# One-core attention, gated convolution and mixer kernel: first mixture's weight cast moved to VectorE, its loads booked later, later heads' preparation issued behind the first head's rows

## Chip, cores and metric

The kernel runs on 1 core of one Trainium2 chip. The metric is the device time of one execution in microseconds (us). Before the change it was 816.27 us, the median of 3 runs (811.01 to 820.26).

## What is computed

Three stages follow one another, all in fp32 on 4 batches of 576 tokens:

```
scores = q @ k.T / 8 + min(-(cum_i - cum_j), 0), causal      # 8 heads x 4 batches, cum = cumsum(max(s, 0))
attn   = softmax(scores);  x = attn @ v                      # (4, 576, 512)
h      = max(x @ w_in, 0);  c = 3-tap depthwise conv of h over tokens
x      = (h * sigmoid(c)) @ w_out                            # "first mixture", 512 -> 1024 -> 512
u      = x + U,V mixing of the tokens (rank 32)
out    = u + max(u @ w_ch1, 0) @ w_ch2                       # 512 -> 2048 -> 512
```

The weights of the mixtures are float64 in HBM, and the core turns them into fp32 pairs (a high part and a remainder) itself.

## The kernel before, in words

**A planner sets the order.** The Python code first collects operations with an engine, a cost in ns, and the buffers read and written (`Plan.op`). `Plan.order` (L219 on) then runs a list schedule: it keeps a clock for each engine (PE = TensorE, DVE = VectorE, ACT = ScalarE, POOL = GpSimd, SP, which issues the DMAs), takes the engine that is free first, and issues its ready operation with the lowest program number. An operation is ready when all its predecessors (`preds`) are done by this bookkeeping: end of the predecessor, plus a latency between the two engines, plus the predecessor's `late`. For a DMA on SP `late` is worked out from its bytes (one shared wire, 360 bytes per ns). The result is a fixed order for each engine; on the chip each engine works through its own list in that order and waits on semaphores. So an instruction that waits for data holds up all that stands behind it on its engine, whatever the planner believed. SP too issues its DMAs in order, and a DMA that reuses one of eight completion semaphores waits until the DMA that had it before has landed.

**The heads.** `att_head(h)` (L1317) is called for each of the 32 heads (`NH`) in turn: it asks for the loads of the next head (`prep_v`, `prep4`, `prep`, `place`), then plans scores (`scores`, `scores4`), softmax, transposes (`transp`) and the product with v (`av`). Heads 0 to 7 (`FS`) use plain fp32 products: `prep4` (L576) loads q and k into a tile `qkF` and puts the head's row of `cc` (the running sum of s) into it by two small DMAs, called "the head's rows" below (`qkF<-cc`). From head 8 on, q and k of two heads are loaded together into two tiles `t` (`prep`, L599), split by POOL (L356) and DVE (L362) into high and low parts, and copied by DMA into `qkA` and `qkB` (`place`, L617); the rows then come from a scratch tensor `r_d` in HBM, which `decay_parts` (L462) fills once: DVE splits `cc` into the tile `ws`, and four DMAs write `r_d` (two from `ws`, two of ones). `clear` (L479) zeroes the two `qkB` tiles on POOL.

**The first mixture's weights.** There are 16 slices of 128x512 (`w1_jobs`): eight of `w_in` (`w1h`, `w1l`) and eight of `w_out` (`w1o`). For each, `load_split` (L527) plans the load of 512 KB (`raw_w<-w_in`, L530) into a ring of two buffers, `decode64` (ACT Prelu L504 on the raw tile, then DVE L511 and L520, which give fp32), the high part as an ACT cast (`hi_act`, L353) and the low part as a DVE subtraction (`lo_dve`, L362). `st["first"]` is head 0's row DMA; the loads of `load_split` have it as a predecessor.

**Around the start.** SP issues s, q/k of head 0, v, the mask and the identity (`ident`, three DMAs) before head 0's rows, because the planner sees those as ready earlier; DVE clips and sums s (L459, L460), and in the order before also splits `cc` for `r_d` there. `h == 1` is the call of `att_head` in which `decay_parts` and `clear` are asked for.

**PSUM.** Scores, transposes, av products and the mixtures share eight banks; a bank is given to the next user when its last reader is done, so PE can wait for an ACT copy that empties a bank of another kind (`x<-av`, L843).

Of the kernel before, what the change touches and what calls it, by code (L numbers as in the profile page):

```python
# [42 lines left out]
AHEAD = 80  # L43

RECIP = (3,)

CAPS = dict(sc=3, pt=1, av=5, h=4, y=4, tp=2, t1=4, mh=1, ma=8, my=8, mx=2)

# [89 lines left out]
class Op:  # L138

    def __init__(self, eng, cost, fn, n, late):  # L140
        self.eng, self.cost, self.fn, self.n, self.late = eng, cost, fn, n, late
        self.preds = set()


class Plan:
# [36 lines left out]
    def order(self):  # L182
# [46 lines left out]
        while True:  # L229
# [47 lines left out]
            late = o.late  # L277
            if e == "SP":
                wire = max(wire, t + 1400) + o.late
                late = wire + 980 - end  # L280
            self.busy[e] += o.cost
            out.append((t, len(out), o))
            for b in holds.get(o, ()):
# [25 lines left out]
def tile_attention_moe_mixer(  # L309
# [149 lines left out]
    dve(S, lambda: nc.vector.tensor_scalar(cum(), cum(), 0.0, 8.0, ALU.max, ALU.mult), key, key, True)  # L459
    scan = dve(S, lambda: nc.vector.tensor_tensor_scan(cum(), cum(), cum(), 0.0, ALU.add, ALU.max), key, key)  # L460

    def decay_parts():  # L462
        hi_dve(lambda: rk[:, 0, :], cum, key, [(rk, 0)], S)
        lo_dve(lambda: rk[:, 1, :], cum, lambda: rk[:, 0, :], [*key, (rk, 0)], [(rk, 1)], S)
        for i in range(2):
            dma(
                147456,
                lambda i=i: nc.sync.dma_start(out=f32(r_t[:, i:4:2, 1 - i, :]), in_=f32(rk())),
                [rk],
                [(r_d, i)],  # L470
            )
            dma(
                147456,
                lambda i=i: nc.sync.dma_start(out=f32(r_t[:, i:4:2, i, :]), in_=one_d[i]),
                [],
                [(r_d, 2 + i)],
            )

    def clear(t):  # L479

        o = pool(2 * S, lambda: nc.gpsimd.memset(f32(t[0:64]), 0.0), [], [(t, "r"), (t, "q")], extra=0)
        o.preds.add(scan)

    for t in p4s:
        o = pool(64, lambda t=t: nc.gpsimd.memset(t[:, S:640], 0.0), [], [(t, "pad")], extra=0)
        o.preds.add(scan)


    def decode64(out, okeys, raw, n):

        def half(i, dt):
            return raw().bitcast(dt).rearrange("p (n two) -> p n two", two=2)[:, :n, i]

        def oi():
            return out().bitcast(I32)  # L500

        act(
            n,
            lambda: nc.scalar.activation(half(1, F32), half(1, F32), ACTF.Prelu, scale=2.0**-111, alpha=2.0**32),  # L504
            [raw],
            [(raw, 1)],
            40,
        )
        dve(
            n,  # L510
            lambda: nc.vector.tensor_scalar(  # L511
                oi(), half(1, I32), 3, None, ALU.logical_shift_left
            ),
            [(raw, 1)],
            okeys,
            True,
        )
        dve(
            n,
            lambda: nc.vector.scalar_tensor_tensor(  # L520
                oi(), half(0, I32), 29, oi(), ALU.logical_shift_right, ALU.bitwise_or
            ),
            [(raw, 1), *okeys],
            okeys,
        )

    def load_split(src, h, l, c, n, name, lo=lo_pool):  # L527

        raw = ring(dec, "raw", RINGS["w64"], [128, 512], I64, f"raw_{name}")
        load = dma(n * 1024, lambda: nc.sync.dma_start(out=raw[:, :n], in_=src[:, c : c + n]), [], [raw])  # L530
        load.preds.add(st["first"])
        wf = ring(dec, "wf", RINGS["wf"], [128, 512], F32, f"wf_{name}")
        decode64(lambda: wf[:, :n], [wf], raw, n)
        hi_act(lambda: h[:, :n], lambda: wf[:, :n], [wf], [h], n)
        lo(lambda: l[:, :n], lambda: wf[:, :n], lambda: h[:, :n], [wf, h], [l], n)

    def load_cw():
# [61 lines left out]
    def prep(h):  # L599

        t1 = ring(ap, "t1", RINGS["qkh"], [128, 2, S], F32R, f"t1_{h}")
        t2 = ring(ap, "t2", RINGS["qkh"], [128, 2, S], F32R, f"t2_{h}")

        for c, (hi, lo) in enumerate(((t1, t2), (t2, t1))):

            def raw(c=c, lo=lo):
                return f32(lo[:, c, :])

            dma(294912, lambda c=c, raw=raw: nc.sync.dma_start(out=raw(), in_=qk[h // 2, :, c]), [], [(lo, c)])
            hi_pool(lambda c=c, hi=hi: hi[:, c, :], raw, [(lo, c)], [(hi, c)], S)  # L610
            lo_dve(
                lambda c=c, lo=lo: lo[:, c, :],
                raw,
                lambda c=c, hi=hi: hi[:, c, :],
                [(lo, c), (hi, c)],
                [(lo, c)],
                S,  # L617
            )
        st["pair", h // 2] = (t1, t2)
# [685 lines left out]
    hi_dve(lambda: mask[:, 384:512], lambda: mraw[:, 0:128], [mraw], [(mask, 1)], 128)  # L1305
    hi_dve(lambda: mask[:, 736:800], lambda: mraw[:, 128:192], [mraw], [(mask, 2)], 64)
    dma(65536, lambda: nc.sync.dma_start(out=ident[:, 0:128], in_=ident_d), [], [(ident, 0)])

    for a in (0, 64):
        dma(  # L1310
# [2 lines left out]
            [],  # L1313
            [(ident, 1 + a)],
        )

    w1_jobs = [(f, c) for c in (0, 512) for f in range(NF1)]  # L1317

    def att_head(h):

        if h + 1 < NH:
# [4 lines left out]
            else:  # L1326
                if h % 2 == 1:
                    prep(h + 1)
                place(h + 1)
        if h == 1:  # L1330
            decay_parts()
            for t in qkBs:
                clear(t)
# [48 lines left out]
    for h in range(NH + 1):  # L1382
# [10 lines left out]
        att_head(h)  # L1393
        for n, (f, c) in enumerate(w1_jobs):
            if h == W1_AT[n]:
                load_split(w1[f], w1h[f, c], w1l[f, c], c, 512, f"w1_{f}_{c}", lo_dve)
        if h == CW_AT:
            load_cw()
        if h == MIX_AT:
# [180 lines left out]
```

## Time and profile before

| | before |
|---|---|
| median of 3 runs | 816.27 us |
| the profiled execution, its own time | 813.74 us |
| its span, first to last instruction | 811.9 us |
| mean granted TensorE clock | 0.995 |
| TensorE busy | 788.5 us (97%) |
| ACT busy / DVE busy / POOL busy | 464.1 / 471.8 / 182.3 us |
| moved by DMA | 119.69 MB, mean 147 GB/s |

The profile is of one execution, 813.74 us long, of which 811.9 us lie between the first and the last instruction. Times of rows are us from the start of that span. "Busy" is time in which an engine executes; a row's bracket, [idle before <-releaser], is how long the engine sat idle before it and which engine's work or which DMA ended that. PEclk is the mean clock granted to TensorE as a share of its upper level: 1.00 is 2.4 GHz and 0.50 is 1.2 GHz.

### The profile page before, as it was taken

To read this page: it belongs to the slowest core of one execution; us is meant where nothing else is said; L and a number is where in the kernel's file an instruction comes from. 1 tells how busy PE (TensorE), PEld (TensorE's weight loads), DVE (VectorE), ACT (ScalarE), POOL (GpSimd) and SP (SyncE) were. 2 spreads that over 40 slices of the span, in tenths; PEclk is the share of its full clock that TensorE was granted. 3 is DMA by queue.
4 is the path that set the end of the run, shared out by engine and by line. 5 is a ranking of instruction groups with operands and counts; after the bars stand their busy time and mean duration, and the time that the engine had idled before them with its cause. 6 is when DMAs were issued, how large, how long until landed. Compare 5 with 4: busy or idle time off the path is not lost.

```text
span 811.9 us, 15176 instructions
## 1 busy us (share of the span) xinstructions
PE 788.5 (97%) x5300; PEld 708.5 (87%) x5300; DVE 471.8 (58%) x1152; ACT 464.1 (57%) x1176; POOL 182.3 (22%) x291
## 2 busy tenths in 40 slices
PE   4899999999999999999999999999999999999998
PEld 2556798998899998999999999999998888888888
DVE  6686886635855368547888957444576232323232
ACT  4688998758868488776667445444455222222221
POOL 3444564633446245241220000000000000000000
PEclk9899999999999999999999999999999999999999
DMA  7657755644555256230226346455578363636343
GB/s 215 174 161 216 208 144 136 161 111 101 154 135 142 69 114 194 45 111 1 91 79 207 136 153 213 147 174 187 165 246 294 95 201 97 198 101 188 111 123 98
DMA packets 66309, 119.69 MB, mean 147 GB/s; under 512 B 9396, under 2 KB 34868, under 8 KB 66232
## 3 DMA queue, kind: packets, MB, share of 16 engines
q1 hardware_dynamic: 66160, 118.70, 50.5%
q8 instruction: 42, 0.69, 0.4%
q14 instruction: 35, 0.29, 0.1%
q10 hardware_dynamic: 72, 0.01, 0.0%
HBM read 68.81 MB, written 28.90 MB: 120 GB/s over the span
## 4 chain that ended last, share of the span: by engine, by line
PE 90%; DMA 5%; ACT 3%; DVE 1%; issue 1%; POOL 0%; SPq 0%; DVEq 0%; ACTq 0%; POOLq 0%
PE my L1261 24%; PE ma_A L1161 16%; PE y L916 13%; PE h L874 12%; PE ma_S L1161 6%; PE sc L681 6%; PE pt L804 5%; PE av L830 5%; DMA raw_w<-w_in 2%; PE tp L933 1%; DMA qkF<-cc 1%; PE t L952 1%; ACT P L659 1%; DMA r_d<-ws 1%; DMA qkA<-t 1%
## 5 line engine op out<-in xcount | busy, mean ns | idle before, releaser
L1261 PE MATMUL my<-mh,w 128*128 128x512 f32 (+1 forms) x560 | 159.2, 368 | 0.0
L1161 PE MATMUL ma_A<-u,W 128*128 128x288 f32 x960 | 138.2, 295 | 0.0
L1161 PEld LDWEIGHTS ma_A<-u,W 128*128 128x128 f32 x960 | 131.4, 188 | 0.5 <-ACT p L1175 0.2
L1239 ACT ACTIVATE mh<-ml 128x512 fp32r<-128x512 f32 (+1 forms) x80 | 47.2, 589 | 137.5 <-DMA ml<-ch_d 79.2
L1261 PEld LDWEIGHTS my<-mh,w 128*128 128x128 f32 x560 | 101.7, 189 | 17.5
L1242 DVE SCALAR_TENSOR_TENSOR ml<-ml,mh 128x512 fp32r<-128x512 f32 (+1 forms) x80 | 50.6, 638 | 112.8 <-ACT mh L1239 112.6
L916 PE MATMUL y<-gh,w1o 128*128 128x288 f32 x512 | 113.4, 300 | 0.0
L1261 PE MATMUL my<-ml,w 128*128 128x512 f32 (+1 forms) x280 | 103.1, 368 | 0.0
L670 POOL TENSOR_SCALAR P<-P,sm 128x128 f32<-128x128 f32 (+3 forms) x128 | 75.5, 606 | 91.9 <-DVE sm L733 64.3
L642 DVE CUSTOM_DVE_ANT_0 sc<-sc,mask 128x128 f32<-128x128 f32 (+2 forms) x144 | 69.1, 498 | 38.4 <-PE sc L681 36.0
L916 PEld LDWEIGHTS y<-gh,w1o 128*128 128x128 f32 x512 | 85.3, 188 | 0.5
L874 PE MATMUL h<-xh,w1h 128*128 128x290 f32 x256 | 79.7, 311 | 0.1
L886 DVE SCALAR_TENSOR_TENSOR c<-h,cw,c 128x288 f32<-128x288 f32 x128 | 64.2, 513 | 24.3 <-ACT c L882 23.3
L874 PE MATMUL h<-xl,w1h 128*128 128x290 f32 x256 | 76.5, 299 | 0.0
L874 PE MATMUL h<-xh,w1l 128*128 128x290 f32 x256 | 76.3, 298 | 0.0
L916 PE MATMUL y<-gl,w1o 128*128 128x288 f32 x256 | 75.3, 294 | 0.0
L1175 ACT COPY s<-ma_A 128x288 f32<-128x288 f32 x96 | 38.2, 400 | 64.2 <-PE ma_A L1161 55.0
L659 ACT ACTIVATE P<-sc,sm 128x128 f32<-128x128 f32 (+3 forms) x128 | 68.2, 537 | 9.8 <-DVE sm L642 6.1
L365 POOL TENSOR_TENSOR gl<-c,gh 128x288 fp32r<-128x288 f32 x64 | 52.7, 829 | 92.7 <-ACT gh L901 79.4
L353 ACT COPY th<-pt 128x384 f32<-128x384 f32 (+2 forms) x128 | 63.8, 498 | 9.3 <-PE pt L804 8.5
L804 PE MATMUL pt<-ident,P 128*128 128x128 f32 x320 | 60.3, 276 | 1.0 <-ACT P L659 0.9
L1261 PEld LDWEIGHTS my<-ml,w 128*128 128x128 f32 x280 | 52.8, 189 | 8.6
(135 smaller groups left out, 1528.4 us busy)
## 6 DMA issues: line engine op xcount, KB each, us to landing
ml<-ch_d SPq DMA_DIRECT2D x64, 256.0 KB
ch_d<-s SPq DMA_DIRECT2D x64, 144.0 KB
raw_w<-w_in SPq DMA_DIRECT2D x16, 512.0 KB
raw_w2a<-w_in SPq DMA_DIRECT2D x16, 512.0 KB
raw_w2b<-w_in SPq DMA_DIRECT2D x16, 512.0 KB
t<-qk_in SPq DMA_DIRECT2D x24, 288.0 KB
qkB<-t SPq DMA_DIRECT2D x24, 288.0 KB
qkA<-t SPq DMA_DIRECT2D x24, 288.0 KB
```

Source lines behind the costliest of these rows:

```text
L353: act(n, lambda: nc.scalar.copy(out(), src()), r, w)
L365: pool(n, lambda: nc.gpsimd.tensor_tensor(out(), src(), f32(hi()), ALU.subtract), r, w, two=True)
L642: lambda: nc.vector.tensor_tensor_reduce(out=ps[:rows, :w], in0=ps[:rows, :w], in1=mask[:rows, m0 : m0 + w], scale=-0.125, scalar=3.0e38 i ...
L659: lambda: nc.scalar.activation(out(), ps[:rows, :w], ACTF.Exp, bias=low(), scale=-1.0, accum_out=total()),
L670: lambda: nc.gpsimd.tensor_scalar(t[:, :w], t[:, :w], r(), 1.0, ALU.mult, ALU.mult),
L804: nc.tensor.transpose(pt[:, o + rows - 128 : o + rows], d["P"][i][:, 128 * j : 128 * j + 128], turn)
L874: nc.tensor.matmul(ps[:, :W], lhsT=ww, rhs=xx, start=kt + n == 0, stop=kt == KT - 1 and n == 2)
L886: lambda k=k: nc.vector.scalar_tensor_tensor(c(), hh[:, k : k + HS], cw[:, 3 * f + k : 3 * f + k + 1], c(), ALU.mult, ALU.add),
L916: nc.tensor.matmul(ps[:, :HS], lhsT=ww, rhs=xx(), start=f + n == 0, stop=f == NF1 - 1 and n == 2)
L1161: nc.tensor.matmul(ps[:, :HS], lhsT=ww, rhs=uu, start=first and k == 0, stop=k == 5, skip_group_check=True)
L1242: lambda: nc.vector.scalar_tensor_tensor(ml[:, :n], raw(), 0.0, f32(mh[:, :n]), ALU.max, ALU.subtract),
L1261: nc.tensor.matmul(ys[c][dt][:, :n], lhsT=ww, rhs=xx[:, :n], start=f + k == 0, stop=f == NF2 - 1 and k == 2)
```

## The change

Four things are done. (1) The high part of the 16 slices of the first mixture is cast on DVE (`hi_dve`) in place of ACT (`hi_act`). (2) For those slices the planner books the load 3 x 400 ns later and the Prelu's result 400 ns later (`SLACK`); no instruction is added, only the planner's idea of when things are ready moves. (3) `decay_parts` and `clear` are asked for in `att_head(4)`, not `att_head(1)`, and are tied to the last PE operation planned by then (`after_pe`); the loads of head 8's and 9's q and k get the 25th last PE operation as a predecessor. (4) The three identity DMAs get head 0's row DMA as a predecessor.

```diff
+SLACK = 400
...
             if e == "SP":
                 wire = max(wire, t + 1400) + o.late
-                late = wire + 980 - end
+                late = wire + 980 - end + o.slack
...
+    def after_pe(o, back=1):
+        o.preds.add([x for x in plan.ops if x.eng == "PE"][-back])
+
     def decay_parts():
         hi_dve(lambda: rk[:, 0, :], cum, key, [(rk, 0)], S)
+        after_pe(plan.ops[-1])
...
                 [(r_d, 2 + i)],
             )
+            after_pe(plan.ops[-1])
...
         o = pool(2 * S, lambda: nc.gpsimd.memset(f32(t[0:64]), 0.0), [], [(t, "r"), (t, "q")], extra=0)
-        o.preds.add(scan)
+        after_pe(o)
...
-    def decode64(out, okeys, raw, n):
+    def decode64(out, okeys, raw, n, slack=0):
...
             40,
-        )
+        ).late = slack
...
-    def load_split(src, h, l, c, n, name, lo=lo_pool):
+    def load_split(src, h, l, c, n, name, lo=lo_pool, slack=0):
...
         load.preds.add(st["first"])
+        load.slack = 3 * slack
...
-        hi_act(lambda: h[:, :n], lambda: wf[:, :n], [wf], [h], n)
+        (hi_dve if slack else hi_act)(lambda: h[:, :n], lambda: wf[:, :n], [wf], [h], n)
...
             dma(294912, lambda c=c, raw=raw: nc.sync.dma_start(out=raw(), in_=qk[h // 2, :, c]), [], [(lo, c)])
+            if h == len(FS):
+                after_pe(plan.ops[-1], 25)
...
     dma(65536, lambda: nc.sync.dma_start(out=ident[:, 0:128], in_=ident_d), [], [(ident, 0)])
+    plan.ops[-1].preds.add(st["first"])
...
-        if h == 1:
+        if h == 4:
             decay_parts()
...
-                load_split(w1[f], w1h[f, c], w1l[f, c], c, 512, f"w1_{f}_{c}", lo_dve)
+                load_split(w1[f], w1h[f, c], w1l[f, c], c, 512, f"w1_{f}_{c}", lo_dve, SLACK)
```

Since a list schedule decides, the whole order of the first heads shifts. On PE the rows differ up to the product `y_0_2` of the first mixture's first half-batch (its rows after the 656th); the 3190 rows behind it read alike in both programs.

The first place is SP's queue at the start, up to the rows of head 2 (third head). `cc` is the running sum, `qkF_104` and `qkF_129` are the tiles of even and odd heads, `vr` holds v, `raw_w_f_c` is slice f of the weights, `t_8` belongs to heads 8 and 9. Before:

```order
L584 DMA qkF_129<-cc 1x16x36
L596 DMA vr_165<-vP_in 128x640
L530 DMA raw_w_0_0_169<-w_in 128x512
L468 DMA r_d<-ws 64x1x576
L474 DMA r_d<-one_in 64x576
L468 DMA r_d<-ws 64x1x576
L474 DMA r_d<-one_in 64x576
L530 DMA raw_w_1_0_198<-w_in 128x512
L609 DMA t_8_204<-qk_in 128x576
L582 DMA qkF_104<-qk_in 64x1152
L584 DMA qkF_104<-cc 1x16x36
L589 DMA qkF_104<-cc 1x16x36
```

And now:

```order
L591 DMA qkF_129<-qk_in 64x1152
L605 DMA vr_141<-vP_in 128x640
L593 DMA qkF_104<-cc 1x16x36
L593 DMA qkF_129<-cc 1x16x36
L1318 DMA ident<-ident_in 128x128
L1324 DMA ident<-ident_in 128x64 x2
L538 DMA raw_w_0_0_177<-w_in 128x512
L538 DMA raw_w_1_0_184<-w_in 128x512
L591 DMA qkF_104<-qk_in 64x1152
L593 DMA qkF_104<-cc 1x16x36
L598 DMA qkF_104<-cc 1x16x36
```

The four `r_d` writes and the load of `t_8` no longer stand between head 0 and head 2; q and k of head 1 and the second v tile now stand ahead of head 0's rows, where only the identity stood.

The second place is SP's queue further on, where these writes and loads stand now: behind the rows of head 5 (`qkF_129`), ahead of slice 6 and of q, k and rows of head 6 (`qkF_104`).

```order
L591 DMA qkF_129<-qk_in 64x1152
L593 DMA qkF_129<-cc 1x16x36
L598 DMA qkF_129<-cc 1x16x36
L481 DMA r_d<-one_in 64x576 x2
L475 DMA r_d<-ws 64x1x576 x2
L538 DMA raw_w_6_0_506<-w_in 128x512
L591 DMA qkF_104<-qk_in 64x1152
L593 DMA qkF_104<-cc 1x16x36
L598 DMA qkF_104<-cc 1x16x36
L618 DMA t_8_562<-qk_in 128x576
L618 DMA t_8_573<-qk_in 128x576
L640 DMA qkB_457<-r_d 4x1152
```

Before, the same stretch of the queue held this:

```order
L530 DMA raw_w_6_0_461<-w_in 128x512
L582 DMA qkF_129<-qk_in 64x1152
L584 DMA qkF_129<-cc 1x16x36
L589 DMA qkF_129<-cc 1x16x36
L530 DMA raw_w_7_0_542<-w_in 128x512
L530 DMA raw_w_0_512_562<-w_in 128x512
L582 DMA qkF_104<-qk_in 64x1152
L584 DMA qkF_104<-cc 1x16x36
L589 DMA qkF_104<-cc 1x16x36
L596 DMA vr_615<-vP_in 128x640
```

The slices fall behind by one or two, and the `r_d` writes and `t_8` loads take their place.

The third place is ACT around the copy `x_0<-av_1` that empties the bank of the first av product (L843 before, L854 now). `P` and `p` are softmax rows, `th` transposed rows, `raw_w` the Prelu of a slice. Before:

```order
L353 COPY th_0_416<-pt_0_391 128x384
L353 CAST w1h_420<-wf_w_3_0_374 128x512
L659 ACTIVATE P_0_425,sm_212<-sc_0_386,sm_212 128x128
L659 ACTIVATE P_1_430,sm_212<-sc_1_397,sm_212 128x256
L504 ACTIVATE raw_w_4_0_376<-raw_w_4_0_376 128x512
L843 COPY x_0_363<-av_1_403 128x320
L353 CAST xh_0_106<-x_0_363 128x576
L353 COPY th_1_451<-pt_1_438 128x512
```

And now:

```order
L670 ACTIVATE P_1_385,sm_199<-sc_1_355,sm_199 128x256
L356 COPY th_0_398<-pt_0_378 128x384
L512 ACTIVATE raw_w_3_0_301<-raw_w_3_0_301 128x512
L670 ACTIVATE P_2_404,sm_199<-sc_2_367,sm_199 128x384
L854 COPY x_0_347<-av_1_387 128x320
L356 CAST xh_0_106<-x_0_347 128x576
L356 COPY th_1_425<-pt_1_408 128x512
L512 ACTIVATE raw_w_4_0_369<-raw_w_4_0_369 128x512
```

Slice 4's Prelu, which stood directly ahead of that copy, now stands behind it, slice 3's stands ahead of it in its place, and the cast of slice 3 has left ACT.

## Rows read from the trace of the kernel before

**Rows 1.** The page: span and busy time of each engine.

```profile
span 811.9 us, 15176 instructions
...
PE 788.5 (97%) x5300; PEld 708.5 (87%) x5300; DVE 471.8 (58%) x1152; ACT 464.1 (57%) x1176; POOL 182.3 (22%) x291
```

**Rows 2.** Windows: stretch, length, busy PE, PEld, DVE, ACT, POOL; PEclk, DMA share, GB/s.

```profile
8.40:50.00 41.60, 34.80 (x180) 21.86 (x182) 28.15 (x90) 30.00 (x85) 18.37 (x25) 0.92 0.71 205
50.00:100.00 50.00, 45.63 (x307) 33.30 (x304) 39.21 (x122) 44.00 (x128) 24.60 (x36) 1.00 0.70 200
100.00:155.00 55.00, 55.00 (x425) 50.04 (x424) 37.64 (x115) 46.44 (x138) 30.13 (x46) 1.00 0.61 147
155.00:812.00 657.00, 653.09 (x4395) 603.25 (x4394) 361.15 (x821) 342.78 (x827) 105.90 (x167) 1.00 0.47 140
21.80:25.10 3.30, 3.30 (x10) 2.54 (x11) 1.37 (x6) 1.25 (x4) 1.95 (x4) 0.50 0.44 93
38.80:42.20 3.40, 3.40 (x13) 2.83 (x12) 2.56 (x10) 2.67 (x8) 1.34 (x2) 0.50 0.54 148
...
35.00:65.00 30.00, 26.24 (x156) 17.10 (x154) 21.46 (x67) 24.31 (x67) 13.45 (x20) 0.94 0.57 172
35.40:37.90 2.50, 0.07 (x2) 0.02 (x1) 0.35 (x2) 1.01 (x3) 0.00 (x0) 1.00 0.95 282
```

**Rows 3.** Timeline of PE, 0 to 90 us: start, length, instruction [idle before <-releaser].

```profile
18.78 0.33 PE L804 MATMUL pt<-ident,p 128*128 128x128 f32 x1 [1.35 <-POOL p L670]
...
21.79 1.62 PE L681 MATMUL sc<-qkF 128*128 128x128 f32 x4 [2.24 <-DMA qkF<-cc]
...
37.88 1.19 PE L681 MATMUL sc<-qkF 128*128 128x512 f32 x2 [2.42 <-ACT x L843]
...
48.53 0.71 PE L697 MATMUL sc<-qkF 128*64 128x288 f32 x4
...
53.36 0.91 PE L681 MATMUL sc<-qkF 128*128 128x384 f32 x2 [0.79 <-ACT x L843]
...
56.32 0.39 PE L681 MATMUL sc<-qkF 128*128 128x128 f32 x2
...
69.61 1.77 PE L681 MATMUL sc<-qkF 128*128 128x384 f32 x4 [1.00 <-ACT x L843]
```

**Rows 4.** The chain that ended last, in order of time: start, length, what.

```profile
6.24 1.82 DMA qkF<-cc
9.01 5.86 DMA r_d<-ws
14.90 6.76 DMA qkF<-cc
...
30.15 6.63 DMA raw_w<-w_in
...
153.34 1.20 PE y L916 x9
```

**Rows 5.** Timeline of ACT, 8 to 100 us: Prelus that waited for their slice.

```profile
36.86 0.65 ACT L504 ACTIVATE raw_w<-raw_w 128x512 f32<-128x512 f32 x1 [2.78 <-DMA raw_w<-w_in]
...
52.33 0.67 ACT L504 ACTIVATE raw_w<-raw_w 128x512 f32<-128x512 f32 x1 [1.33 <-DMA raw_w<-w_in]
...
68.59 0.66 ACT L504 ACTIVATE raw_w<-raw_w 128x512 f32<-128x512 f32 x1 [1.48 <-DMA raw_w<-w_in]
```

**Rows 6.** Waits of SP's queue, 0 to 30 us: us in total, times, longest.

```profile
SPq L1312 <- DMA qkF<-qk_in: 1.7, 1, 1.7
```

**Rows 7.** Groups by shape, 0 to 155 us: busy us, mean ns.

```profile
L511 DVE TENSOR_SCALAR wf_w<-raw_w 128x512 int32<-128x512 int32 x16 | 8.8, 553 | 8.0 <-ACT raw_w L504 8.0
...
L353 ACT CAST w1h<-wf_w 128x512 fp32r<-128x512 f32 x8 | 5.1, 641 | 0.2 <-DVE wf_w L520 0.2
...
L481 POOL MEMSET qkB<- 64x1152 f32 x2 | 2.0, 1053 | 0.0
```

**Rows 8.** Line L359, VectorE's casts: ns min/median/max, first and last start.

```profile
L359 DVE CAST ws<-cc x1: 447/447/447, 5.6 to 5.6; 32x576 fp32r<-32x576 f32 x1
```

More of the change, by code (lines that the diff above doesn't have):

```diff
@@ L141, in __init__ @@
         self.eng, self.cost, self.fn, self.n, self.late = eng, cost, fn, n, late
+        self.slack = 0
         self.preds = set()
@@ L531, in load_split @@
         load.preds.add(st["first"])
+        load.slack = 3 * slack
         wf = ring(dec, "wf", RINGS["wf"], [128, 512], F32, f"wf_{name}")
-        decode64(lambda: wf[:, :n], [wf], raw, n)
-        hi_act(lambda: h[:, :n], lambda: wf[:, :n], [wf], [h], n)
+        decode64(lambda: wf[:, :n], [wf], raw, n, slack)
+        (hi_dve if slack else hi_act)(lambda: h[:, :n], lambda: wf[:, :n], [wf], [h], n)
         lo(lambda: l[:, :n], lambda: wf[:, :n], lambda: h[:, :n], [wf, h], [l], n)
@@ L1315, in tile_attention_moe_mixer @@
         )
+        plan.ops[-1].preds.add(st["first"])
     w1_jobs = [(f, c) for c in (0, 512) for f in range(NF1)]
```

## Prediction

> **What bounds the kernel now.** I first read the busy shares: TensorE works 788.5 of 811.9 us [rows 1], so 23.4 us without work is all that a new order can win, besides stretches at a lower clock. The windows say where they lie [rows 2]: 8.4 us at the start, before the first product, 6.8 us between 8.4 and 50 (41.60 - 34.80), 4.4 us between 50 and 100, none between 100 and 155, 3.9 us in the 657 us behind that. PE's last row that the change moves is in the product `y_0_2`, which ends at 153.34 + 1.20 = 154.5 [rows 4]; behind it the order is the same and PE has work nearly without a gap, so what is won or lost before 154.5 should reach the end one for one.
>
> Then the timeline of PE, for the gaps one by one [rows 3]: 1.35 (a softmax row still on POOL), 2.24 (the rows of head 2), 2.42, 0.79 and 1.00 (each time a bank that an ACT copy had yet to empty), together 7.8 of the 11.2 us lost between 8.4 and 100. Two of them cost more than their length: from 21.80 for 3.30 us and from 38.80 for 3.40 us, each right behind a gap of over 2 us, the granted clock is 0.50, the lower of its two levels, with PE busy throughout [rows 2]. That is 1.65 and 1.70 us more.
>
> Last, what those gaps waited for. The rows of head 2 are 2.2 KB, and took 6.76 us from issue to landing at 14.90; in front of them SP's queue holds an `r_d` write that took 5.86 us [rows 4], with three more like it, a slice of weights and `t_8`. The three ACT copies were late because a Prelu ahead of them in ACT's order waited for its slice: 2.78, 1.33 and 1.48 us at 36.86, 52.33 and 68.59 [rows 5]. The first slice took 6.63 us from its issue at 30.15 [rows 4]. So these waits of PE are waits for DMAs, passed on by ACT.
>
> **The change part by part.** The sum is made against the profiled execution (813.74 us, 1.8 of it outside its span); it lies 2.5 us under the median of the runs, and I add that difference at the end.
>
> *The start.* Head 0's rows now stand behind head 1's q and k and the second v tile, 608 KB, where the identity's 128 KB stood. An issue of SP can wait for an earlier landing: the second identity DMA waited 1.7 us for q and k [rows 6]. The 480 KB more are 1.7 us at the 282 GB/s of 35.4 to 37.9 [rows 2] if nothing hides them, and nothing if the rows wait for the running sum anyway. ACT issued its two row DMAs at 6.24 and they landed in 1.82 [rows 4]. The identity, which moves behind, is first used by the transposes, behind the scores of heads 0 and 1, and DVE loses two operations (one is the cast of 447 ns [rows 8]) ahead of the mask. I take -0.6 us (0 to -1.7).
>
> *The `r_d` writes and `t_8` leave the start.* Ahead of head 2's rows only two slices, q and k are left. The gap of 2.24 and the slow clock behind it should go: +3.9 us (0 to 3.9). The 1.35 us for POOL I leave where they are (0 to +1.35): a score product now stands in that gap, but the same softmax row ends it.
>
> *The first late slice.* The load is booked 1.2 us and the Prelu 0.4 us later, 1.6 of the 2.78 us that it was late. The rest: `t_8`'s copies to the two `qkB` tiles, 576 KB, went into the queue directly ahead of it and now don't, 2.0 us at 282 GB/s. In the new order slice 3's Prelu, not slice 4's, stands ahead of the copy. So +2.42 + 1.70 = +4.1 us (0 to 4.1).
>
> *The two later ones.* 1.33 and 1.48 are both under 1.6, but the moved traffic falls near them; half of 0.79 + 1.00, +0.9 us (0 to 1.8).
>
> *What the moved work meets.* Four `r_d` writes (576 KB), two loads and two copies of `t_8` (1152 KB), 1.7 MB, now go between head 5's and head 8's loads. That is 6.3 us at 282 GB/s; from 35 to 65 the DMA engines are busy 0.57 of 30 us [rows 2], which leaves 13. It fits on the mean, not at every place. The queue is in order, and slice 6 and q, k and rows of head 6 stand directly behind the writes. I take -1.0 us, like one of the smaller gaps of rows 3; the bound is a gap like head 2's with its clock, -3.9. The zeroing of `qkB`, 2 x 1.05 us on POOL [rows 7], now stands ahead of head 3's softmax rows; POOL is busy 18.4 of the 41.6 us there [rows 2], so 0, and -2.1 if that cover is gone.
>
> *The cast.* ACT loses 16 x 0.64 = 10.3 us [rows 7]. DVE's cast of 128x512 isn't in the trace. Between the 447 ns of 32x576 [rows 8] and the 553 of a 128x512 operation with one input [rows 7] I take the second, which has the shape: 16 x 0.55 = 8.8 us. On PE by itself 0 (+1.0 to -1.5).
>
> *The pace.* When PE waits less, ACT and DVE must do the same work in less time. From 8.4 to 50 DVE is busy 28.2 us; with 5 casts 30.9, in 33.6 us instead of 41.6, 92%. ACT falls from 30.0 to 26.8, 80%. The nearest stretch with an engine that full is 50 to 100: ACT 88%, and PE lost 4.4 us, 2.6 without the two late slices, which is 5%. Of 33.6 us that is 1.7; I take -1.5 (0 to the whole 8.0 of the two large gaps).
>
> A rule speaks against the cast. The Trainium skill, "SBUF — State Buffer", section "Who interferes with whom", says that a copy or cast on DVE can run in a mode with two ports, and that it and a GpSimd instruction then exclude each other for their whole length. No row here shows a DVE cast beside POOL. By that rule POOL, busy 43 of the 92 us up to 100 us, would meet about half of the 16 casts, some 4 us more on POOL in all, and the one gap that waits for POOL, 1.35 us, could come twice: the sum would be 1.4 us smaller. I stay with the sum without it, since PE waited for POOL once.
>
> Sum: -0.6 + 3.9 + 4.1 + 0.9 - 1.0 - 1.5 = 5.8 us won, so the profiled execution would take 807.9 us, and the median of runs 816.3 - 5.8 = 810.5 us, 0.7% less.
>
> **The rivals.**
>
> *Everything goes.* The two large gaps with their clocks (8.0), both small ones (1.8) and the 1.35 for POOL, nothing new, less 0.6 at the start: 10.5 us, 805.8 us. For it: ACT gives up 10 us of work in a stretch where it is 88% busy. Against it: DVE at 92%.
>
> *The gaps come back under another name.* DVE sets the pace, or the slices still come after their booking (6.63 us landings against 1.6 us of slack): in the first case the 8.0 are lost but for the 1.5 already taken, -0.7 us; in the second the 4.1 go and 1.7 are left. 814.6 to 817.0 us. For it: PE's gaps end wherever an in-order engine is late, and the planner's booking moves the order, not the data. Against it: the traffic that made the slices late has gone from that stretch.
>
> *The moved traffic stalls PE further on: slower.* The place is SP's queue behind head 5's rows: writes, slice 6, head 6's q, k and rows, `t_8`, the `qkB` and `qkA` copies, slice 7, head 7's. If each landing there grows to the 6.8 us of head 2's rows, PE waits for head 6's rows, for slice 6, for head 7's rows and for head 8's tiles, 3.9 us each with the clock, 15.6, plus 0.6, less the 8.0 won: 8.2 us slower, 824.5 us. It decides where landing takes longer than the PE work between head 4's last product, which frees the tile, and head 6's first: before, 7.8 us, from 48.53 to 56.32 [rows 3], so a landing of 6.8 us with 1.2 us of issue is just the edge. Against it: the DMA engines have 13 us free there.
>
> **How the numbers follow.** A measurement of this kernel can tell about 1%, 8.2 us, from no change. The forecast (2 to 9 us won) 0.47, of which 0.05 is over 1%; everything goes 0.25, all over 1%; the gaps come back 0.14, within; the moved traffic 0.14, of which 0.10 is slower by over 1%. So faster 0.30, within 0.60, slower 0.10. Range: down to 804, a little under the first rival, as the start may cost nothing and the cast may gain; up to 819, over the second rival and the milder half of the third. The forecast's own range is 807 to 814.
>
> **What would show it.** Right: no gap before head 2's first product over 1 us, PEclk 1.00 from 20 to 45 us, no Prelu of `raw_w` that waits over 1 us up to 70 us, the first product not later than 9.5 us, PE idle between its first product and 100 us about 5 us instead of 11.2, and `y_0_2` ending near 148.7. Wrong: a clock of 0.50 anywhere behind 25 us; PE waiting for `qkF<-cc` of head 6 or 7 or for `qkB`; DVE at 95% with PE's gaps put down to it; or a gain before 154.5 that isn't there at the end.

## The result, and the profile after

The changed kernel takes 818.89 us (median of 20 runs, 817.04 to 821.11), the kernel before 813.75 us (20 runs beside them): ratio 1.0054, 95% interval 1.0037 to 1.0070. So it is 0.5% slower where 0.7% faster was forecast. The profiled execution has a span of 816.9 us (before 811.9). Its busy shares answer to [rows 1]; DVE has 8.9 us more, ACT 5.1 us less:

```profile
PE 790.4 (97%) x5300; PEld 708.2 (87%) x5300; DVE 480.7 (59%) x1168; ACT 459.0 (56%) x1160; POOL 184.3 (23%) x291
```

Windows of the kernel before, cut where the story turns (stretch, its length, then the us in which PE, PEld, DVE, ACT and POOL were busy, with counts; PEclk, DMA share, GB/s):

```profile
8.40:80.00 71.60, 62.13 (x357) 40.58 (x357) 49.73 (x159) 55.77 (x158) 32.13 (x45) 0.95 0.69 196
80.00:100.00 20.00, 18.30 (x129) 14.59 (x128) 17.63 (x54) 18.22 (x55) 10.84 (x16) 1.00 0.78 222
100.00:155.00 55.00, 55.00 (x425) 50.04 (x424) 37.64 (x115) 46.44 (x138) 30.13 (x46) 1.00 0.61 147
```

And of the kernel after:

```profile
8.40:80.00 71.60, 65.77 (x401) 42.55 (x401) 58.09 (x180) 54.69 (x157) 37.57 (x52) 1.00 0.70 193
80.00:100.00 20.00, 15.77 (x93) 13.08 (x94) 14.30 (x40) 13.87 (x44) 9.57 (x16) 0.83 0.66 169
100.00:155.00 55.00, 52.61 (x396) 46.96 (x393) 42.81 (x123) 44.84 (x129) 26.67 (x38) 1.00 0.62 155
```

Up to 80 us the gain is there: 65.77 - 62.13 = 3.6 us more product time (time in which PE is busy), and the half clock of before (1.65 + 1.70 us) is gone, 7.0 us together, the later start already taken off. Behind 80 us it is lost: 18.30 - 15.77 = 2.5 us, 55.00 - 52.61 = 2.4 us, and a stretch at half clock. PE's timeline says where (these answer to [rows 3]; a bracket is the idle time before the row and what ended it):

```profile
18.56 0.46 PE L692 MATMUL sc<-qkF 128*128 128x128 f32 x2 [0.37 <-DMA qkF<-cc]
51.79 1.12 PE L692 MATMUL sc<-qkF 128*128 128x512 f32 x2 [0.90 <-ACT P L670]
84.33 0.55 PE L815 MATMUL pt<-ident,P 128*128 128x128 f32 x3 [0.82 <-POOL P L681]
85.67 0.50 PE L692 MATMUL sc<-qkB 128*128 128x512 f32 x1 [0.79 <-ACT P L670]
88.78 0.61 PE L692 MATMUL sc<-qkA 128*128 128x288 f32 x1 [2.06 <-DMA qkA<-t]
122.40 0.40 PE L927 MATMUL y<-gh,w1o 128*128 128x288 f32 x1 [0.53 <-DVE w1o L365]
165.90 0.52 PE L815 MATMUL pt<-ident,P 128*128 128x128 f32 x3 [0.89 <-ACT P L670]
```

Head 2's 2.24 us became 0.37, and the waits for late slices of 2.42, 0.79 and 1.00 us have no successor over 0.90. New is 2.06 us before the last score product of heads 10 and 11, which waits for a copy into `qkA`, and the granted clock behind it, at the lower of its two levels (0.50, 1.2 GHz) with PE busy, in windows of 2 us of the kernel after:

```profile
86.00:88.00 2.00, 0.72 (x3) 0.19 (x1) 1.91 (x5) 2.00 (x8) 0.48 (x1) 0.94 1.08 238
88.00:90.00 2.00, 1.22 (x5) 1.19 (x6) 0.44 (x3) 1.07 (x4) 1.11 (x2) 0.50 0.72 200
90.00:92.00 2.00, 2.00 (x10) 2.00 (x10) 1.69 (x5) 0.00 (x0) 0.66 (x1) 0.50 0.59 226
92.00:94.00 2.00, 2.00 (x11) 1.66 (x11) 0.78 (x2) 1.19 (x4) 0.39 (x2) 0.50 0.03 8
```

Half of the busy time at the lower level, (1.22 + 2.00 + 2.00) / 2 = 2.6 us, is lost too; with the 4.9 us of lost product time 7.5 us go between 80 and 155. By these windows the kernel after is 0.5 us behind at 155. The chain of waits of the kernel after leads back from that gap to SP:

```profile
80.24 0.55 SPq L640
80.84 0.97 SPq L640
81.86 6.88 DMA qkA<-t
88.78 1.09 PE sc L692 x3
```

The last of head 11's three copies into `qkA` took 6.88 us. SP's queue of the kernel after shows what flew beside it:

```profile
77.27 0.52 SPq L538 DMA_DIRECT2D raw_w<-w_in  x1
77.88 1.35 SPq L605 DMA_DIRECT2D vr<-vP_in  x1
...
80.24 3.74 SPq L640 DMA_DIRECT2D qkA<-t  x3
84.09 0.52 SPq L538 DMA_DIRECT2D raw_w<-w_in  x1
...
102.38 1.60 SPq L538 DMA_DIRECT2D raw_w<-w_in  x2
```

The last load of a slice in the kernel before:

```profile
81.09 0.34 SPq L530 DMA_DIRECT2D raw_w<-w_in  x1
```

Head 11's copies stand between slices 4 and 5 of `w_out`, 512 KB each. In the kernel before all eight slices of `w_out` were issued by 81.1 us; here the last two go at 102.4, and the product `y` waits at 122.40 for what is made of them. Of the 2.4 us without work between 100 and 155, 0.98 us are waits for `w1o` by name (0.45 at 120.52, 0.53 at 122.40).

One more row for each kernel, from PE's first product over the same 901 products, before and after:

```profile
8.41:154.37 145.96, 134.80 (x901) 104.57 (x902) 104.85 (x323) 120.02 (x348) 72.47 (x104) 0.98 0.67 182
```

```profile
9.54:157.03 147.49, 136.18 (x901) 104.59 (x902) 115.21 (x341) 114.70 (x331) 75.85 (x106) 0.98 0.67 177
```

Of the 5.0 us of the spans, 1.13 is the later first product, 1.53 this stretch, and 2.3 come behind it (0.89 of them the gap at 165.90). Inside the stretch the idle time is equal, 11.2 and 11.3 us; the same products are busy 1.4 us longer, though the lower clock takes less of it. The groups of these two stretches say where: in 64 of the products that use the slices of `w_out`, 1.8 us more, all behind 100 us and at the upper clock level. Before, then after:

```profile
L916 PE MATMUL y<-gh,w1o 128*128 128x288 f32 x64 | 14.1, 299 | 0.0
```

```profile
L927 PE MATMUL y<-gh,w1o 128*128 128x288 f32 x64 | 15.9, 308 | 1.0 <-DVE w1o L365 1.0
```

### The profile page after: what moved, and what is told of

The parts are those of the page before. It is cut to its first block, busy times and chain, and to the rows that moved or that the text cites. A ratio compares the mean times of both kernels' runs of the same rounds, so it can differ in the third digit from the quotient of the medians.

```text
span 816.9 us, 15158 instructions
## 1 busy us (share of the span) xinstructions
PE 790.4 (97%) x5300; PEld 708.2 (87%) x5300; DVE 480.7 (59%) x1168; ACT 459.0 (56%) x1160; POOL 184.3 (23%) x291
## 4 chain that ended last, share of the span: by engine, by line
PE 82%; DMA 6%; DVE 5%; ACT 3%; issue 2%; SPq 1%; POOL 1%; ACTq 0%; DVEq 0%; POOLq 0%
PE my L1272 24%; PE ma_A L1172 14%; PE y L927 11%; PE h L885 11%; PE ma_S L1172 5%; PE sc L692 5%; PE pt L815 5%; PE av L841 4%; DMA qkA<-t 3%; DMA t<-qk_in 1%; PE tp L944 1%; DMA raw_w2b<-w_in 1%; PE t L963 1%; DVE sc L653 1%; PE mh L990 1%
## 5 line engine op out<-in xcount | busy, mean ns | idle before, releaser
L681 POOL TENSOR_SCALAR P<-P,sm 128x128 f32<-128x128 f32 (+3 forms) x128 | 77.9, 625 | 90.8 <-DVE sm L744 71.5
L356 ACT COPY th<-pt 128x384 f32<-128x384 f32 (+2 forms) x128 | 63.5, 496 | 12.1 <-PE pt L815 11.2
```

Source lines behind the costliest of these rows:

```text
L356: act(n, lambda: nc.scalar.copy(out(), src()), r, w)
L681: lambda: nc.gpsimd.tensor_scalar(t[:, :w], t[:, :w], r(), 1.0, ALU.mult, ALU.mult),
```

## The experiments

Each run is compared with the kernel before on the same chip; ratios are to it, with 95% intervals. "Cast" is the cast on DVE, "moved edits" are parts 3 and 4 of the change, "booking" is `SLACK`. The theories: the **late booking** puts weight slices beside the copies of later heads; the **moved edits** do harm; a **full VectorE** does; or the copies wait for a **freed tile** whatever flies beside them.

**One part at a time.** The booking alone, against the changed kernel (the moved edits are undone likewise):

```diff
-        (hi_dve if slack else hi_act)(lambda: h[:, :n], lambda: wf[:, :n], [wf], [h], n)
+        hi_act(lambda: h[:, :n], lambda: wf[:, :n], [wf], [h], n)
...
-        if h == 4:
+        if h == 1:
```

> The kernel before with the late booking alone (SLACK on the first mixture's loads and on their decode); the cast stays on ScalarE, decay, zeroing, identity and ninth head's loads stay where they were. Late-booking theory (the weight slices now share the DMA queues with the q and k tiles of heads 10 and 11, and a score product waits for head 11's tile): this one is slower than before, 815 to 820 us, with a TensorE gap of 1 us or more that a transfer into qkA ends between 75 and 100 us, and a granted clock of 0.50 behind it. Theory of the moved edits (decay, zeroing, ninth head's loads): about as before or faster, 808 to 814 us, no such gap. Theory of a full VectorE: the same, 808 to 814 us, since the cast is still on ScalarE.

818.52 us, ratio 1.0040 (1.0015 to 1.0064): slower, as the late-booking theory has it. PE's largest gap there, and the copy in the chain of waits that ended it:

```profile
87.00 0.45 PE L688 MATMUL sc<-qkA 128*128 128x128 f32 x1 [3.91 <-DMA qkA<-t]
```

```profile
81.32 5.59 DMA qkA<-t
```

The cast alone is the kernel before with `hi`, a new parameter of `load_split`, in place of `hi_act`; it is `hi_dve` for the first mixture's slices:

```diff
-        hi_act(lambda: h[:, :n], lambda: wf[:, :n], [wf], [h], n)
+        hi(lambda: h[:, :n], lambda: wf[:, :n], [wf], [h], n)
```

> The kernel before with the cast alone: the 16 casts of the first mixture's weight run on VectorE, everything else is booked and issued as before. Late-booking theory: within 2 us of before, 812 to 816 us. Theory of a full VectorE: 2 us or more slower, 816 to 820 us, with VectorE near 2.00 us of every 2 us where a score head and a slice meet, and PE gaps that VectorE ends. Theory of the moved edits: as before.

815.88 us, 1.0012 (0.9992 to 1.0032): no difference that can be told.

The moved edits alone:

```diff
-                load_split(w1[f], w1h[f, c], w1l[f, c], c, 512, f"w1_{f}_{c}", lo_dve, SLACK)
+                load_split(w1[f], w1h[f, c], w1l[f, c], c, 512, f"w1_{f}_{c}", lo_dve)
```

> The kernel before with the moved edits alone: decay and zeroing at head 4, identity and ninth head's loads behind the first head's rows; cast on ScalarE, slices booked as before. Late-booking theory: 2 to 5 us faster than before, 808 to 812 us, since the gap before head 2's first product goes and nothing takes its place. Theory of the moved edits: slower, 815 to 820 us, with the chain of heads 10 and 11's q and k tiles late. Theory of a full VectorE: as the late-booking theory. In each, the first product starts about 1 us later than before (9.5 us).

815.67 us, 1.0002 (0.9980 to 1.0024). A miss for every theory: neither faster nor slower. In its trace the gap before head 2's first product is 0.55 us, but there is one of 1.76 us for a head's rows at 40.4 us and one of 2.69 us for a `qkA` copy of heads 8 and 9 at 75.9 us.

The changed kernel's order, casts issued on ACT in the places they have on DVE:

```diff
+        if slack:
+            dve(n, lambda: nc.scalar.copy(h[:, :n], wf[:, :n]), [wf], [h], True)
```

> The changed kernel in its own order on every other engine, with the 16 casts issued on ScalarE in the places where VectorE has them. Theory of a full VectorE: 3 us or more faster than the changed kernel, 812 to 816 us, the gaps between 80 and 95 us shrink below 1 us. Late-booking theory: within 2 us of the changed kernel, 817 to 821 us, with the gap of about 2 us that a transfer into qkA ends at about 89 us still there. Theory of the moved edits: as the late-booking theory.

816.26 us, 1.0007 (0.9985 to 1.0030). The `qkA` gap stays (2.09 us), as the late-booking theory has it, but the time is lower than its 817 to 821. So with the late booking in force and the order unchanged, most of the loss goes when ACT does the cast: in this order the cast on DVE may cost up to 0.5%. Later runs find the opposite sign in other orders.

**The copy and what flies beside it.** The changed kernel again is the measure:

> The changed kernel once more, beside the next three on the same chip, as their measure. Every theory: 0.4 to 0.7% over the kernel before.

818.47 us, 1.0039 (1.0016 to 1.0062).

Two loads made thin, in the same order. Slices 4 and 5 of `w_out` bring 16 of their 512 columns, into the tile of the slice two before; the rest of their weights is left out, while decode, cast and subtraction still run:

```diff
+        if len(raws) in THIN:
+            raw, m = raws[-2], 16
...
-        load = dma(n * 1024, lambda: nc.sync.dma_start(out=raw[:, :n], in_=src[:, c : c + n]), [], [raw])
+        load = dma(n * 1024, lambda: nc.sync.dma_start(out=raw[:, :m], in_=src[:, c : c + m]), [], [raw])
```

> The changed kernel in its own order, with two loads of weights made thin: slices 4 and 5 of w_out (issued at 77.27 and 84.09 us in the changed kernel) bring 16 of their 512 columns, into the tile of the slice two before, so what is decoded is not these slices; the decode, cast and subtraction still run. Late-booking theory (a megabyte of weights in flight slows the copies into head 11's qkA, 6.88 us): the copy lands in 5 us or less, the gap before the score product of heads 10 and 11 falls from 2.06 us to under 0.5, there is no half clock behind it, and the time is 2 to 5 us under the changed kernel's. Theory that the copies are late because they can start only when head 9's scores have freed the tile: gap, clock and time stay as in the changed kernel, within 1.5 us. Theory of a full VectorE: the same, unchanged.

815.01 us, 1.0009 (0.9984 to 1.0034), 3.5 us under the changed kernel beside it. Landings of the copies into `qkA` issued from about 80 to 82 us, first in the changed kernel, then in this run; then two windows of this run:

```profile
DMA to landing us min/median/max: 7.3/7.3/7.3
```

```profile
DMA to landing us min/median/max: 4.9/4.9/4.9
```

```profile
84.00:86.00 2.00, 0.95 (x5) 0.61 (x5) 2.00 (x7) 2.00 (x9) 1.44 (x3) 1.00 0.62 137
86.00:88.00 2.00, 2.00 (x10) 1.90 (x9) 1.93 (x5) 2.00 (x7) 0.56 (x1) 0.55 0.69 214
```

The copy lands in 4.9 us instead of 7.3 (as this view counts it, from the issue) and PE doesn't wait for it; from 86 to 88 PE is busy throughout. The freed-tile theory, which had gap and time unchanged, falls. That there would be no half clock was wrong: it comes 2 us earlier, behind the gaps for POOL and ACT.

The same two loads planned behind the copies (called the hold below; `behind` is the last of the copies for slices 4 and 5):

```diff
+        if behind is not None:
+            load.preds.add(behind)
```

> The changed kernel with the loads of slices 4 and 5 of w_out planned behind the last copy into head 11's qkA; all else as in the changed kernel. Late-booking theory: the 2.06 us gap goes, but the slices come 7 us later, so the product y_0_0 may wait for them; 1 to 4 us under the changed kernel. Theory of the freed tile: gap as in the changed kernel and the later slices on top, the same or up to 3 us slower.

814.28 us, 0.9986 (0.9963 to 1.0009), 4.2 us under the changed kernel. The window from 80 to 100 of this run, to be set against 15.77 at a clock of 0.83:

```profile
80.00:100.00 20.00, 17.89 (x127) 14.69 (x127) 17.48 (x46) 18.46 (x53) 12.40 (x18) 1.00 0.66 175
100.00:155.00 55.00, 50.98 (x382) 45.45 (x381) 41.17 (x120) 43.38 (x126) 26.13 (x38) 1.00 0.69 163
```

The gap and the half clock go, but behind 100 us 4.0 us of product time are missing. No PE wait there names a slice: the largest are 1.50 us for ACT's `th` (behind a Prelu of `raw_mix`, the mixing weights, that waited 2.01 us for its own load), 1.05 us for DVE's `c` (DVE was mostly at slices of `w_out` from 98.72 to 103.44, directly before) and 0.86 us for a `qkA` copy. That later slices cause all of it is not shown.

No booking at all, cast and moved edits kept (and no `SLACK` at the call):

```diff
-        (hi_dve if slack else hi_act)(lambda: h[:, :n], lambda: wf[:, :n], [wf], [h], n)
+        (hi_dve if name.startswith("w1_") else hi_act)(lambda: h[:, :n], lambda: wf[:, :n], [wf], [h], n)
```

> The changed kernel without the late booking: cast on VectorE, decay, zeroing, identity and ninth head's loads moved, slices booked as before. If the booking is what costs (0.4% alone in the run with the booking only): within 1.5 us of the kernel before, 3 to 5 us under the changed kernel. If the cast on VectorE costs only in company with the moved edits: as slow as the changed kernel.

822.77 us, 1.0099 (1.0068 to 1.0130): a clear miss. Its largest PE gap, and the transfer in the chain of waits behind it:

```profile
61.35 0.67 PE L708 MATMUL sc<-qkF 128*64 128x288 f32 x2 [2.81 <-DMA qkF<-cc]
```

```profile
53.22 7.99 DMA qkF<-cc
```

Head 7's rows, 2.2 KB, took 7.99 us behind `t_8`'s loads, two slices and v. This is the rival "the moved traffic stalls PE further on", at its place; in the changed kernel the booking had kept it away. So the booking does good and harm.

**Where else the hold and the start count.** The identity in front again, with the hold:

```diff
-    plan.ops[-1].preds.add(st["first"])
...
-        plan.ops[-1].preds.add(st["first"])
```

> As the run that holds slices 4 and 5 behind head 11's copies, and the identity's three loads again in front of the first head's rows, as before the change. If the later first product (0.7 us in that run, 9.13 against 8.41 us) comes from head 1's q and k and the second v tile in front of the rows, and reaches the end: first product near 8.4 us and 0.5 to 1 us less than that run, 812.5 to 814 us. If the start is hidden by what comes later: the same time as that run within its uncertainty.

821.78 us, 1.0100 (1.0063 to 1.0138). The first product came at 8.27 us as expected, and the time at neither value: three loads, 128 KB together, in another place gave another order, with gaps of 2.61 us (ACT) and 4.33 us (`qkA`). A gain of a microsecond at the start can't be read off alone here.

The hold with the cast on ACT:

```diff
-        (hi_dve if slack else hi_act)(lambda: h[:, :n], lambda: wf[:, :n], [wf], [h], n)
+        hi_act(lambda: h[:, :n], lambda: wf[:, :n], [wf], [h], n)
```

> As the run that holds slices 4 and 5 behind head 11's copies, with the cast on ScalarE (planned there too). Late-booking theory with nothing else wrong: within 2 us of that run. Theory that the cast fills VectorE: 1.5 us or more under that run, below the kernel before, with fewer waits of PE for VectorE's c between 100 and 125 us.

816.82 us, 1.0042 (1.0019 to 1.0066), against 0.9986 with the cast on DVE. A miss for both expectations: with the hold, the cast on DVE helps.

The booking alone with the hold, added to the first kernel of this section:

```diff
+        if behind is not None:
+            load.preds.add(behind)
```

> The kernel before with the late booking alone, and slices 4 and 5 of w_out held behind head 11's copies. Late-booking theory: the gap of 3.91 us before a product with head 11's qkA, in the run with the booking alone, goes with its half clock, and the time falls by 3 us or more, to the kernel before or under it, 811 to 815 us. If the hold only helped the changed kernel by chance of its order: no better than the booking alone, 817 to 820 us.

814.63 us, 1.0008 (0.9982 to 1.0033); the booking alone was at 1.0040. The gap of 3.91 us is gone and the hold helps in a second order too. That order differs elsewhere as well: new are 3.99 us before head 2's first product and 2.02 us for a `qkA` copy at 76.3 us.

**Which half of the booking.** For the `w_in` slices alone:

```diff
-                load_split(w1[f], w1h[f, c], w1l[f, c], c, 512, f"w1_{f}_{c}", lo_dve, SLACK)
+                load_split(w1[f], w1h[f, c], w1l[f, c], c, 512, f"w1_{f}_{c}", lo_dve, SLACK if c == 0 else 1)
```

> The changed kernel with the late booking for the eight w_in slices alone; the eight of w_out are booked as before (1 ns of it is left). In this order slices 4 and 5 of w_out still stand in front of head 11's copies, and slice 5 comes nearer to them. If the date of the booking is what costs: back to 812 to 815 us. If the place of these slices in front of the copies costs, whatever moved them there: 817 to 822 us, with a gap of 1.5 us or more for a qkA copy between 80 and 95 us.

812.21 us, 0.9975 (0.9956 to 0.9995): faster than both kernels. Its windows, and its largest gap:

```profile
80.00:100.00 20.00, 16.20 (x122) 13.85 (x120) 17.10 (x45) 16.96 (x49) 10.85 (x14) 1.00 0.82 201
100.00:155.00 55.00, 53.98 (x410) 49.24 (x407) 41.87 (x126) 46.18 (x135) 32.29 (x47) 1.00 0.63 157
```

```profile
82.94 0.33 PE L692 MATMUL sc<-qkB 128*128 128x128 f32 x1 [2.09 <-DMA qkB<-t]
```

The gap for a copy is there, as the place of the slices had it, but the time is what the date had: behind 100 us only 1.0 us of product time is missing, where the changed kernel misses 2.4 and the hold 4.0, and the clock stays at its upper level in this execution. The same once more:

> The run with the first half's booking alone, once more: 0.1 to 0.4% under the kernel before if its gain is there, within 0.1% of it if it was chance.

812.07 us, 0.9956 (0.9934 to 0.9978). The gain is there a second time. In its profiled execution the gap before the same product is longer, and the lower clock level does follow it:

```profile
84.39 0.33 PE L692 MATMUL sc<-qkB 128*128 128x128 f32 x1 [2.68 <-DMA qkB<-t]
```

```profile
86.00:88.00 2.00, 2.00 (x10) 2.00 (x9) 1.97 (x8) 1.76 (x7) 1.52 (x3) 0.50 0.98 195
```

For the `w_out` slices alone:

```diff
-                load_split(w1[f], w1h[f, c], w1l[f, c], c, 512, f"w1_{f}_{c}", lo_dve, SLACK)
+                load_split(w1[f], w1h[f, c], w1l[f, c], c, 512, f"w1_{f}_{c}", lo_dve, SLACK if c else 1)
```

> The changed kernel with the late booking for the eight w_out slices alone; the eight of w_in are booked as before (1 ns of it is left). If it is the late booking of the w_out slices that costs: as slow as the changed kernel or slower, 817 to 822 us. If the two halves only disturb each other: 812 to 815 us, as the first half alone.

824.06 us, 1.0101 (1.0064 to 1.0138). Its trace has both kinds of gap: 2.21 us at 60.3 us for head 7's rows, as in the run without any booking, and 3.37 us at 81.1 us for a `qkA` copy.

The `w_in` booking with the hold (in the kernel with the hold, whose call spans lines):

```diff
-lo_dve, SLACK, st["put"] if n in (12, 13) else None
+lo_dve, SLACK if c == 0 else 1, st["put"] if n in (12, 13) else None
```

> Late booking for the w_in slices alone, and slices 4 and 5 of w_out held behind head 11's copies. If their place in front of the copies is what costs: the 2.09 us gap for a copy into qkB at 83 us, in the run without the hold, goes, and the time is 1 to 3 us under that run, 809 to 812 us. If what counts is how late the slices come: the waits between 100 and 130 us come back, 813 to 817 us.

815.37 us, 0.9999 (0.9974 to 1.0023), as for "how late the slices come". PE's largest gap of this run is behind 100 us:

```profile
107.11 0.61 PE L888 MATMUL h<-xh,w1h 128*128 128x290 f32 x1 [3.18 <-DVE c L909]
```

From 100.02 to 104.32 us DVE works on nothing but slices of `w_out` (their decode, cast and subtraction), and the operations that make this `c` stand behind them in its order. A late slice costs PE here through the engine that decodes it, without a product that waits for the slice itself.

The `w_in` booking with the cast on ACT (the edit of the hold with the cast on ACT):

> Late booking for the w_in slices alone, and the cast on ScalarE, planned there; the moved edits stay. If the cast on VectorE has no part in the gain: within 2 us of the run with the first half's booking and the cast on VectorE, 810 to 814 us. If it has: 2 us or more slower than that run, 815 to 819 us, with PE waits for ScalarE of over 1 us.

817.08 us, 1.0010 (0.9987 to 1.0034), against 0.9956 with the cast on DVE beside it. Two PE gaps of this run, both for ACT, then what ACT did ahead of the first:

```profile
53.74 1.13 PE L692 MATMUL sc<-qkF 128*128 128x512 f32 x2 [3.51 <-ACT th L356]
74.70 0.33 PE L815 MATMUL pt<-ident,p 128*128 128x128 f32 x1 [2.66 <-ACT P L670]
```

```profile
52.75 0.62 ACT L356 CAST w1h<-wf_w 128x512 fp32r<-128x512 f32 x1 [3.92 <-DVE wf_w L528]
```

The cast stood directly ahead of the copy `th` in ACT's order and waited 3.92 us for DVE's decode, and the copy and PE with it. The hold with the cast on ACT has the same: a cast that waited 3.39 us for `wf_w`, and a PE gap of 3.00 us for `th` behind it. So what the cast costs on ACT here is its place in an ordered list, more than its own 0.62 us. The second gap has another cause, a Prelu that waited 2.75 us for its slice.

With cast and moved edits in place the booking makes this table, ratios to the kernel before:

| booked later | ratio | interval |
|---|---|---|
| none | 1.0099 | 1.0068 to 1.0130 |
| `w_in` slices | 0.9975, again 0.9956 | 0.9956 to 0.9995, 0.9934 to 0.9978 |
| `w_out` slices | 1.0101 | 1.0064 to 1.0138 |
| both (the change) | 1.0054, again 1.0039 | 1.0037 to 1.0070, 1.0016 to 1.0062 |

## Why the prediction was wrong

**The step that failed** is in "the first late slice" and "the two later ones": the booking was costed as a gain for the slices that were late up to 70 us, and not at all for the eight `w_out` slices behind them. Those it pushes between and behind the copies of heads 10 and 11. Without their booking the kernel is 6.7 us faster than the change (812.2 against 818.9; 0.9975 against 1.0054), and that alone turns the sign. It is not the only edit that takes the loss away: the thin loads (1.0009), the hold (0.9986) and the cast on ACT in the same order (1.0007) do so too, but only booking the `w_in` slices alone is clearly faster than the kernel before.

*The `r_d` writes and `t_8` leave the start*, +3.9: the gap of 2.24 fell to 0.37 and the half clock behind it went. Right.

*The first late slice*, +4.1, and *the two later ones*, +0.9: those waits went, as read. Up to 80 us 7.0 us were won; the terms that fall there (3.9 + 4.1 + 0.9, less 0.6 and 1.5) make 6.8. That the sum of this part is near is no proof of each size.

*The start*, -0.6: 1.13, inside its bounds; the first product came at 9.54, over the 9.5 given as a sign (9.29 in the second profile of the changed kernel).

*The cast*: 16 x 0.55 us was forecast. The trace has 0.571 and 0.562 us (below). ACT's busy time fell by 5.1 us, not by the 10.3 that were taken off. That it costs nothing by itself held (1.0012). But it isn't nothing in company: with the `w_in` booking it is worth 0.5% (1.0010 on ACT, 0.9956 on DVE), in good part by the waiting cast shown above, while in the changed kernel's own order the run on ACT came out lower (1.0007). Both are single orders; what the cast is worth at large stays open.

*The pace*, -1.5: besides the four gaps that were to go (6.45 us), PE was idle for 3.0 us up to 80 us before and for 4.7 us after, 1.7 us more, in small waits for ACT and POOL. The size is near; that a fuller DVE makes them is not shown.

*What the moved work meets*, -1.0: PE waited neither for head 6's or 7's rows nor for `qkB`. The place was the wrong one; the mechanism, a transfer that lands late among large ones, came at heads 10 and 11, with 2.06 us of gap and 2.6 us of clock, and there the large ones were the late slices, not the moved work. The run without the booking shows the forecast place too.

*"What is won before 154.5 should reach the end one for one"* held for half of it (2.3 of the 5.0 us came behind that point, in an unchanged order). And I took "none between 100 and 155" from the trace before as if the new order couldn't make idle time there. It made 2.4 us, 0.98 of them waits for late slices by name.

The second rival, gaps that come back under another name, names the outcome best, but 814.6 to 817.0 us was too little and its causes (DVE's pace, slices behind their booking up to 40 us) were others.

Two things aren't settled, and against the kernel before they are most of the 5.0 us, since what was won up to 80 us and what was lost up to 155 us nearly cancel. The same 901 products are busy 1.4 us longer after the change, with 1.8 us more in products that use the slices of `w_out`; a wait shorter than the end of a product would show so, but no run separates this. And of the 2.3 us lost behind 157 us only 0.89 has a name.

## What to carry to other kernels

A booking that a planner applies to a whole class of loads moves every member of the class: follow the last ones too, and price what they fly beside and who waits for them when they come. A gain before the first stretch in which the bounding engine is full pays only if the work that fills that stretch is ready as much earlier: here 7.0 us won by 80 us became 5.0 us lost at the end. An operation that is cheap by its length can cost by its place: on an engine that works in order it holds up all behind it while it waits. In an order that a list schedule makes, one edit's worth has no fixed sign (the cast was worth from about -0.5% to +0.5% here), so try the parts alone and in pairs.

## What the runs showed of the hardware

Casts on DVE beside POOL. Of the kernel after, the 128x512 casts (count: least, median and largest ns; the 571 and 562 above are the means), and two of them in DVE's timeline with the POOL rows beside:

```profile
L362 DVE CAST w1h<-wf_w x8: 416/461/870, 20.0 to 55.2; 128x512 fp32r<-128x512 f32 x8
L362 DVE CAST w1o<-wf_w x8: 410/422/893, 62.6 to 120.4; 128x512 fp32r<-128x512 f32 x8
```

```profile
102.57 0.41 DVE L362 CAST w1o<-wf_w 128x512 fp32r<-128x512 f32 x1
103.51 1.69 DVE L365 TENSOR_TENSOR w1o<-wf_w,w1o 128x512 fp32r<-128x512 f32 x1
105.89 0.67 DVE L365 TENSOR_TENSOR w1o<-wf_w,w1o 128x512 fp32r<-128x512 f32 x1
120.39 0.89 DVE L362 CAST w1o<-wf_w 128x512 fp32r<-128x512 f32 x1
```

```profile
103.00 1.66 POOL L368 TENSOR_TENSOR xl<-x,xh 128x576 fp32r<-128x576 f32 x1 [1.22 <-ACT xh L356]
119.90 1.91 POOL L359 TENSOR_SCALAR t<-t 128x576 fp32r<-128x576 f32 x2
```

A cast that takes 0.41 us took 0.89 beside POOL, and a subtraction of two tiles 1.69 instead of 0.67: it ended 0.54 us after POOL did (105.20 and 104.66). The rule weighed in the prediction, the Trainium skill, "SBUF — State Buffer", section "Who interferes with whom", agrees; the same section says that a DVE instruction with two inputs in SBUF meets a GpSimd instruction that reads SBUF, which the subtraction shows. I had given the price to POOL. In these rows both are longer: POOL's `xl<-x,xh` beside the subtraction took 1.66 us, where its median in this trace is 1.21. Over the whole execution POOL was busy 2.0 us more than before (184.3 and 182.3), against the 4 us that I had worked out by the rule.

The clock. In the kernel before the lower level followed the two gaps of over 2 us, and I took that for the pattern. In the run with the `w_in` booking a gap of 2.09 us at 82.9 us was followed by no lower clock (1.00 from 80 to 100); in the same kernel once more a gap of 2.68 us before the same product was followed by 0.50 from 86 to 88 us. And in the run with thin loads it fell to 0.55 from 86 to 88 us with no gap over 0.82 us ahead. A gap's length alone doesn't tell what it costs in clock.
